# Constant fills off VectorE, query maxima split in PSUM, tails transposed by TensorE, and loads issued step by step in a fused attention and gated-MLP kernel

## The chip, the cores and the metric

One core of a Trainium2 chip. The metric is device time in microseconds (us) of one execution. A lower time is better. Executions of one kernel vary by a few per cent here, so each comparison below says how many runs stand behind it. A run is called slow when it is over 1.5% above the fastest run of its kernel; fast runs are compared with fast runs. Engines: PE is TensorE, PEld its weight loads, DVE VectorE, ACT ScalarE, POOL GpSimd, SP the sync engine, whose only work here is to issue DMA (a "q" behind a name is its queue of issues).

## The reference

Linear attention over 8 batches of 8 heads, 576 tokens of 64 elements, followed by a gated MLP whose gate mixes tokens.

```python
def phi(x):                                   # attention features
    proj = einsum('bhsd,df->bhsf', x, w_phi)  # 64 -> 128
    proj = proj - max(abs(proj), axis=-1)
    return concatenate([exp(proj), exp(-proj)], axis=-1)
q_p, k_p = phi(q), phi(k)
kv = einsum('bhsf,bhsd->bhfd', k_p, v);  z = sum(k_p, axis=2)
attn = (q_p @ kv) / (q_p @ z + 1e-6)
x = attn as (batch, token, head*64)           # 8 x 576 x 512
u, v = split(relu(x @ w_in));  v_n = layernorm(v)
v_s = einsum('ts,bsd->btd', w_spatial, v_n) + b_spatial
out = (u * v_s) @ w_out
```

## The kernel before

The 576 tokens of a head are 512 ("main") and 64 ("tail"). A **unit** is a pair of heads of one batch (main tokens), or the tails of two batches together (all eight heads). Unit 0 is the first pair of batch 0, unit 1 the first tail, units 2 to 4 the other pairs of batch 0. In step i the kernel works on several units at different stages and fills the gaps with MLP tasks from a queue, which is empty until batch 0 is through. Names of tiles below: k_tl, q_tl and v_tl are loaded tails, k_bf, q_bf and v_f loaded main tokens; kT and qT are their transposes (kT_t, qT_t for tails and kT_b, qT_b for a batch by DMA); mk and mq are the maxima, mhl a maximum in two bf16 parts and mT its transpose; kf and qf are the features (exponentials); em is exp of the key maxima, vs and vst are v and its tails scaled by em; vn and vnt are the normalized v of the MLP and of its tails (vnt has a row of ones, for the bias); xT is the transposed attention output; ob is an output buffer. In some views L61 stands for many places, since it is the line of the helper `pin`.

```python
def load_tail(g):                                  # both tails of a group
    ...
    for x, t in (("k", k), ("q", q)):
        for i in range(2):
            pin(nc.gpsimd.dma_start)(out=d[x][i*TL:(i+1)*TL], in_=tail_ap(t, 2*g + i))
        if 2*g >= XB:                              # all groups but the first
            d[x+"T"] = ld.tile([P, NP, P], BF16, tag=x+"T_t", ...)
            pin(nc.sync.dma_start_transpose)(out=d[x+"T"], in_=d[x]...)
    ...                                            # v by sync

def load(b):                                       # k and q by gpsimd, each with its DMA transpose
    alloc(b); load_heads(b, 0, H)
    load_v(b, nc.gpsimd if b < 2 else nc.sync)
...
for i in range(2):                                 # constants, before the loop
    t = cpool.tile([P, 2, 2, H, DA], BF16, name=f"vst{i}");  nc.vector.memset(t, 0.0)
    t = cpool.tile([P, 2, HALF], BF16, name=f"vnt{i}");      nc.any.memset(t, 0.0)
    ...
def a_queries(u):                                  # maxima of |q features| by VectorE, from PSUM
    u["mq"] = small.tile([P, H], FP32, tag="mq")
    for half in range(2):
        nc.vector.tensor_reduce(out=u["mq"][:, 4*half:4*half+4], in_=by_token(u["qT"], half), ...)
def a_split(u):                                    # fp32 maximum into two bf16 parts
    m = mhl[u["i"] % NM];  eng = nc.vector if u["i"] < EARLY else nc.gpsimd
    eng.tensor_copy(out=m[:, 0:H], in_=u["mq"])
    eng.tensor_tensor(out=m[:, H:2*H], in0=u["mq"], in1=m[:, 0:H], op=ALU.subtract)
...
ORDER = (("keys", 0.375), ("queries", 0), ("sums", 0), ("next", 0.125),
         ("attention", 0.5), ("features", 0), ("maxima", 0), ("out", 0))
RATE = 3.23;  CAP = 1.76                           # how much MLP work goes behind each stage
...
for i in range(NU + 4):
    u = unit(i);  step(i)
    if i == 0: load(1); load_weights()
    if u and u["pair"] and u["pj"] == NP-1 and u["b"]+2 < B: load(u["b"]+2)
    if u and u["pair"] and u["pj"] == TS and u["b"]%2 == TB and u["g"]+1 < G: load_tail(u["g"]+1)
```

Of the kernel before, what the change touches and what calls it, by code (L numbers as in the profile page):

```python
# [16 lines left out]
def kernel(  # L17
# [25 lines left out]
    NB = 4  # L43
# [16 lines left out]
    def pin(start):  # L60
        return lambda **kw: tc.keep_in_program_order(start(**kw))  # L61
# [12 lines left out]
    TS, TB = 1, 1  # L74
    XB = 2

    def load_tail(g):
        d = dict(
            q=ld.tile([P, H, D], BF16, tag="q_tl", name="q_tl", bufs=1),
            k=ld.tile([P, H, D], BF16, tag="k_tl", name="k_tl", bufs=1),  # L80
            v=ld.tile([P, H, D], FP32, tag="v_tl", name="v_tl", bufs=1),
        )
        gs[g] = d
        for x, t in (("k", k), ("q", q)):
            for i in range(2):
                pin(nc.gpsimd.dma_start)(out=d[x][i * TL:(i + 1) * TL], in_=tail_ap(t, 2 * g + i))
            if 2 * g >= XB:
                d[x + "T"] = ld.tile([P, NP, P], BF16, tag=x + "T_t", name=x + "T_t", bufs=1)
                pin(nc.sync.dma_start_transpose)(out=d[x + "T"], in_=d[x].rearrange("p h d -> p (h d)"))
        for i in range(2):  # L90
            pin(nc.sync.dma_start)(out=d["v"][i * TL:(i + 1) * TL], in_=tail_ap(v, 2 * g + i))

    def alloc(b):
        st[b] = dict(
            q=ld.tile([P, H, NB * D], BF16, tag="q_bf", name="q_bf", bufs=2),
            k=ld.tile([P, H, NB * D], BF16, tag="k_bf", name="k_bf", bufs=2),
            v=ld.tile([P, H * NB, D], FP32, tag="v_f", name="v_f"),
        )
        if b >= XB:
            for x in ("kT", "qT"):  # L100
                st[b][x] = ld.tile([P, 2 * H, P], BF16, tag=x + "_b", name=x + "_b", bufs=2)

    def load_heads(b, h0, n):
        d = st[b]
        for x, t in (("k", k), ("q", q)):
            src = d[x][:, h0:h0 + n]
            pin(nc.gpsimd.dma_start)(out=src, in_=main_ap(t, b, h0, n))
            if b >= XB:
                pin(nc.sync.dma_start_transpose)(out=d[x + "T"][:, 2 * h0:2 * (h0 + n), :],
                                            in_=src.rearrange("p h x -> p (h x)"))  # L110
# [4 lines left out]
    def load(b):  # L115
        alloc(b)
        load_heads(b, 0, H)
        load_v(b, nc.gpsimd if b < 2 else nc.sync)


    ident = cpool.tile([P, P], BF16)
    make_identity(nc, ident)
    alloc(0)
    for x, t in (("k", k), ("q", q)):
        first = s2.tile([P, 2, NB * D], FP32, tag="ob", name="first", bufs=4)
        nc.sync.dma_start(out=first, in_=main_ap(t, 0, 0, 2))
        nc.vector.tensor_copy(out=st[0][x][:, 0:2], in_=first)
    wphi2 = cpool.tile([P, 2 * F], BF16)
    nc.vector.memset(wphi2, 0.0)
    wphi_f = cpool.tile([P, F], FP32)  # L130
    for i in range(2):
        r = slice(i * D, (i + 1) * D)
        nc.sync.dma_start(out=wphi_f[r, :], in_=w_phi)
        nc.vector.tensor_copy(out=wphi2[r, i * F:(i + 1) * F], in_=wphi_f[r, :])
    load_tail(0)
    load_heads(0, 2, 2)
    load_v(0, nc.gpsimd)
    load_heads(0, 4, 4)
# [3 lines left out]
    w_spT = cpool.tile([P, NB + 2, S], BF16)  # L142
# [7 lines left out]
    def load_weights():  # L150
        pin(nc.gpsimd.dma_start)(out=w_in_bf, in_=moe_w_in.rearrange("(kc p) f -> p kc f", p=P))
        rows = moe_w_spatial[0:T0, :].rearrange("(p c) s -> p c s", c=NB)
        pin(nc.gpsimd.dma_start)(out=wsp, in_=rows[:, :, 0:T0])
        pin(nc.gpsimd.dma_start)(out=wspr, in_=rows[:, :, T0:S])
        pin(nc.gpsimd.dma_start)(out=wspt, in_=moe_w_spatial[T0:S, :])
        pin(nc.gpsimd.dma_start)(out=w_out_bf, in_=moe_w_out.rearrange("(kc p) f -> p kc f", p=P))


    sel1 = cpool.tile([P, H], BF16)
    sel = cpool.tile([P, H, F], BF16)  # L160
    nc.vector.tensor_tensor(out=sel1, in0=ident[:, 0:H], in1=ident[:, H:2 * H], op=ALU.add)
    nc.vector.tensor_scalar(out=sel, in0=sel1.unsqueeze(2).to_broadcast([P, H, F]), scalar1=-1.0,
                            scalar2=None, op0=ALU.mult)
    neghalf = cpool.tile([P, NB + 1], FP32)
    nc.vector.memset(neghalf, -0.5)


    NM = 3
    EARLY = 4
    XX = 9  # L170
    mhl, mT = [], []
    for i in range(NM):
        t = cpool.tile([P, P], BF16, name=f"mhl{i}")
        nc.vector.memset(t, 0.0)
        mhl.append(t)
        t = cpool.tile([P, P], BF16, name=f"mT{i}")
        nc.vector.memset(t, 0.0)
        mT.append(t)
    vst, vnt = [], []
    for i in range(2):  # L180
        t = cpool.tile([P, 2, 2, H, DA], BF16, name=f"vst{i}")
        nc.vector.memset(t, 0.0)
        vst.append(t)
        t = cpool.tile([P, 2, HALF], BF16, name=f"vnt{i}")
        nc.any.memset(t, 0.0)
        nc.any.memset(t[TL:TL + 1, 0, :], 1.0)
        nc.any.memset(t[0:1, 1, :], 1.0)
        vnt.append(t)
    nc.any.memset(w_spT[:, NB:NB + 2, :], 0.0)

    def transpose_spatial(i):
# [17 lines left out]
        for bl, row in ((0, TL), (1, 0)):  # L209
            for pos, c in enumerate(POS):  # L210
                nc.vector.tensor_copy(out=w_spT[row:row + 1, NB + bl, pos * P:(pos + 1) * P],
                                      in_=bsp_row[row:row + 1, bass.ds(c, P, step=NB)])
            nc.vector.tensor_copy(out=w_spT[row:row + 1, NB + bl, T0:S], in_=bsp_row[row:row + 1, T0:S])


    def a_transpose(u):
# [5 lines left out]
        for x, copy in (("k", nc.scalar.copy), ("q", nc.vector.tensor_copy)):  # L222
            pt = psum.tile([P, 4, P], BF16, tag="bank", name="pt")
            for j in range(4):
                if u["pair"]:
                    blk = src[x][:, 2 * u["pj"] + j // 2, (j % 2) * P:(j % 2 + 1) * P]
                else:
                    blk = src[x][:, 2 * j:2 * j + 2, :]
                nc.tensor.transpose(out=pt[:, j, :], in_=blk, identity=ident)
            u[x + "T"] = a1.tile([P, 4, P], BF16, tag=x + "T", name=x + "T", bufs=2 if x == "k" else 4)  # L230
            copy(out=u[x + "T"], in_=pt)
# [21 lines left out]
    def a_queries(u):  # L253
        u["mq"] = small.tile([P, H], FP32, tag="mq", name="mq")
        for half in range(2):
            pq = by_token(u["qT"], half)
            nc.vector.tensor_reduce(out=u["mq"][:, 4 * half:4 * half + 4], in_=pq, axis=AX.X, op=ALU.max,  # L257
                                    apply_absolute_value=True)

    def a_scale(u):  # L260
        em = small.tile([P, 2, H], FP32, tag="em", name="em")
# [10 lines left out]
        else:  # L272
            d = gs[u["g"]]
            vs = vst[u["g"] % 2]
            for bl in range(2):
                r = slice(bl * TL, (bl + 1) * TL)
                for s in range(2):
                    nc.gpsimd.tensor_tensor(out=vs[r, bl, s, :, 0:D], in0=d["v"][r],
                                            in1=em[r, s, :].unsqueeze(2).to_broadcast([TL, H, D]), op=ALU.mult)
                nc.gpsimd.tensor_copy(out=vs[r, bl, :, :, D:D + 1].rearrange("p i n o -> p i (n o)"), in_=em[r])  # L280
            d["vs"] = vs
            d["unit"] = u

    def a_split(u):
        m = mhl[u["i"] % NM]
        eng = nc.vector if u["i"] < EARLY else nc.gpsimd
        eng.tensor_copy(out=m[:, 0:H], in_=u["mq"])  # L287
        eng.tensor_tensor(out=m[:, H:2 * H], in0=u["mq"], in1=m[:, 0:H], op=ALU.subtract)
# [239 lines left out]
    def unit(i):  # L528
        return units[i] if 0 <= i < NU else None
# [3 lines left out]
    def b_tasks(b):  # L533
# [15 lines left out]
        if tail:  # L549
# [5 lines left out]
            for x in bls:  # L555
# [3 lines left out]
    ORDER = (("keys", 0.375), ("queries", 0), ("sums", 0), ("next", 0.125),  # L559
             ("attention", 0.5), ("features", 0), ("maxima", 0), ("out", 0))  # L560
    RATE = 3.23
    CAP = 1.76
# [10 lines left out]

    def lag(u, what):
        return (FIRST if u["pair"] and u["b"] == 0 or u["i"] == 1 else LAGS).get(what, 0)

    def step(i):
# [3 lines left out]
        for what, share in ORDER:  # L581
            for u in units[max(0, i - 5):i + 2]:
# [8 lines left out]
                elif what == "queries":  # L591
                    a_queries(u)
                    a_split(u)
# [23 lines left out]

    for i in range(NU + 4):
        u = unit(i)
        step(i)  # L620
        if i == 0:
            load(1)
            load_weights()
        if u and u["pair"] and u["pj"] == NP - 1 and u["b"] + 2 < B:
            load(u["b"] + 2)
        if u and u["pair"] and u["pj"] == TS and u["b"] % 2 == TB and u["g"] + 1 < G:
            load_tail(u["g"] + 1)
# [32 lines left out]
```

## Time and profile before

| | before |
|---|---|
| median of 3 runs | 302.22 us (300.67 to 305.91) |
| profiled span | 300.1 us |
| first product with w_in | 53.55 us |
| last group of tail products with w_out starts | 287.67 us |

The prediction below shows the busy times, the first windows and the main waits. Two more views will be compared. The timeline of VectorE, cut to the key maxima `mk` (start, length, engine, line, operation), is a clock of the start: one such group for each unit.

```profile
28.66 1.29 DVE L248 TENSOR_REDUCE mk<-ps 128x4 f32<-128x512 f32 x2
...
48.08 1.29 DVE L248 TENSOR_REDUCE mk<-ps 128x4 f32<-128x512 f32 x2
```

These are units 3 and 7. The view of DMA issues gives size and median time from issue to landing; the first piece of k behind the one that the sync queue loads (two heads, for unit 2) is this one:

```profile
k_bf<-in_k_dram POOLq DMA_DIRECT2D x1, 128.0 KB, 4.0
```

### The profile page before, as it was taken

How to read it: one execution, taken by the hardware profiler on the slowest of the kernel's cores; microseconds unless marked ns; L12 is line 12 of the kernel's file. 1: busy time of each engine (PE TensorE's matmuls, PEld its weight loads, DVE VectorE, ACT ScalarE, POOL GpSimd, SP SyncE). 2: the span in 40 equal slices, each digit the busy share in tenths (PEclk: the TensorE clock that was granted, in tenths of full speed). 3: DMA queues.
4: the chain of work that ended last, by engine and by line, in shares of the span. 5: the costliest groups of instructions: out<-in, count | busy, mean ns of one | idle time of the engine just before them, and what ended most of it. 6: DMA issues, size and time to landing. Idle time of an engine off the chain costs nothing.

```text
span 300.1 us, 7883 instructions
## 1 busy us (share of the span) xinstructions
PE 262.3 (87%) x3007; PEld 180.4 (60%) x3046; DVE 211.9 (71%) x512; ACT 224.1 (75%) x512; POOL 184.1 (61%) x324
## 2 busy tenths in 40 slices
PE   2356888999999999779999995979999999999983
PEld 1235777576766766556667673656767667545441
DVE  5999889797968877549697883656788864445610
ACT  4336899878699997769999675879999837566033
POOL 9398388589635998447879962814988430048300
PEclk9999999999999999999999997999999999999998
DMA  9999999909952899999612999999303202600026
GB/s 142 245 153 268 166 111 159 262 1 123 215 190 75 109 166 233 152 280 162 136 21 28 185 211 224 142 305 235 81 1 37 20 2 69 226 26 0 0 84 233
DMA packets 82906, 41.10 MB, mean 137 GB/s; under 512 B 53490, under 2 KB 77234, under 8 KB 82868
## 3 DMA queue, kind: packets, MB, share of 16 engines
q1 hardware_dynamic: 55524, 27.08, 41.9%
q0 software_dynamic: 27344, 13.51, 33.1%
q8 instruction: 24, 0.39, 0.6%
q14 instruction: 14, 0.11, 0.1%
HBM read 32.85 MB, written 9.44 MB: 141 GB/s over the span
## 4 chain that ended last, share of the span: by engine, by line
PE 56%; DVE 16%; ACT 14%; DMA 8%; issue 3%; SPq 1%; ACTq 0%; DVEq 0%
PE ps L476 9%; PE pv L402 7%; PE pu L455 6%; PE po L499 6%; PE ps L236 6%; DMA out_dram<-ob 5%; ACT kf L251 5%; PE pn L353 3%; DVE mk L248 3%; DVE mq L257 3%; PE pv L333 3%; ACT qf L320 3%; PE pq L303 3%; PE pq L307 3%; PE ps L477 2%
## 5 line engine op out<-in xcount | busy, mean ns | idle before, releaser
L251 ACT ACTIVATE kf<-ps 128x512 bf16<-128x512 f32 x144 | 76.8, 667 | 19.4 <-DVE mk L248 19.1
L320 ACT ACTIVATE qf<-pq 128x512 bf16<-128x512 f32 x128 | 68.0, 667 | 13.6 <-PE pq L307 13.6
L268 POOL TENSOR_TENSOR vs<-v_f,em 128x512 bf16<-128x512 f32 x64 | 65.6, 1047 | 15.7 <-ACT em L263 15.5
L248 DVE TENSOR_REDUCE mk<-ps 128x4 f32<-128x512 f32 x72 | 46.1, 678 | 9.5 <-PE ps L236 9.2
L257 DVE TENSOR_REDUCE mq<-ps 128x4 f32<-128x512 f32 x72 | 46.3, 679 | 3.1 <-PE ps L236 2.7
L501 ACT COPY ob<-po 128x512 f32<-128x512 f32 (+1 forms) x37 | 21.6, 597 | 25.7 <-PE po L499 17.2
L405 DVE BATCH_NORM_STATS2 stats<-vr 128x6 f32<-128x512 bf16 (+1 forms) x37 | 25.2, 685 | 17.6 <-ACT vr L404 17.5
L402 PE MATMUL pv<-w_in_bf,xT 128*128 128x512 bf16 x119 | 31.2, 379 | 2.2 <-DMA xT<-x 1.7
L476 PE MATMUL ps<-w_spT,vn 128*128 128x512 bf16 x117 | 32.3, 379 | 0.6
L455 PE MATMUL pu<-xT,w_in_bf 128*128 128x512 bf16 x120 | 30.8, 379 | 0.7 <-DVE mq L257 0.3
L307 PE MATMUL pq<-mT,sel 128*128 128x128 bf16 x256 | 30.7, 222 | 0.0
L499 PE MATMUL po<-w_out_bf,uT 128*128 128x512 bf16 x121 | 29.7, 379 | 0.4 <-issue 0.2
L479 DVE TENSOR_TENSOR uT<-ps,uT 128x512 bf16<-128x512 f32 x32 | 22.1, 691 | 11.0 <-PE ps L477 9.7
L307 PEld LDWEIGHTS <-sel 128*128 128x128 bf16 x256 | 25.4, 99 | 6.5 <-issue 2.2
L344 DVE TENSOR_TENSOR x<-pn,rc 128x256 bf16<-128x256 f32 x64 | 25.8, 419 | 1.0
L287 POOL CAST mhl<-mq 128x8 bf16<-128x8 f32 x32 | 6.2, 192 | 33.1 <-DVE mq L257 29.3
L404 ACT ACTIVATE vr<-pv 128x512 bf16<-128x512 f32 (+1 forms) x37 | 23.2, 680 | 4.2 <-PE pv L402 3.3
L333 PE MATMUL pv<-vs,kf 128*128 128x66 bf16 x512 | 25.0, 195 | 0.0
L419 POOL TENSOR_SCALAR vn<-vr,rs 128x512 bf16<-128x512 bf16 x32 | 24.3, 772 | 0.8
L333 PEld LDWEIGHTS <-kf 128*128 128x128 bf16 x512 | 23.9, 99 | 1.0
L353 PE MATMUL pn<-kv,qf 128*128 128x66 bf16 x512 | 22.2, 193 | 2.0 <-ACT kf L251 0.9
L353 PEld LDWEIGHTS <-qf 128*128 128x128 bf16 x512 | 19.4, 97 | 6.0 <-issue 2.5
(127 smaller groups left out, 547.5 us busy)
## 6 DMA issues: line engine op xcount, KB each, us to landing
out_dram<-ob SPq DMA_DIRECT2D x32, 256.0 KB, 2.7
v_f<-in_v_dram SPq DMA_DIRECT2D x6, 1024.0 KB, 6.8
k_bf<-in_k_dram POOLq DMA_DIRECT2D x7, 512.0 KB, 6.7
q_bf<-in_q_dram POOLq DMA_DIRECT2D x7, 512.0 KB, 8.3
v_f<-in_v_dram POOLq DMA_DIRECT2D x2, 1024.0 KB, 8.5
v_tl<-in_v_dram SPq DMA_DIRECT2D x8, 128.0 KB, 4.2
w_in_bf<-in_moe_w_in_dram POOLq DMA_DIRECT2D x1, 1024.0 KB, 12.5
out_dram<-ob SPq DMA_DIRECT2D x8, 128.0 KB, 2.9
```

The source lines that it names most:

```text
L248: nc.vector.tensor_reduce(out=u["mk"][:, hs], in_=pk, axis=AX.X, op=ALU.max, apply_absolute_value=True)
L251: nc.scalar.activation(out=u["kf"][:, s, hs, :], in_=pk, func=AF.Exp, bias=0.0, scale=sc)
L257: nc.vector.tensor_reduce(out=u["mq"][:, 4 * half:4 * half + 4], in_=pq, axis=AX.X, op=ALU.max, apply_absolute_value=True)
L268: nc.gpsimd.tensor_tensor(out=vs[:, s, :, 0:D], in0=st[u["b"]]["v"][:, pj * H:(pj + 1) * H, :], in1=em[:, s, :].unsqueeze(2).to_broadcast( ...
L307: nc.tensor.matmul(out=pq[:, 2 * par + x, :], lhsT=sel[:, j, :], rhs=m, start=False, stop=(x == 1))
L320: nc.scalar.activation(out=qf[:, s], in_=pq, func=AF.Exp, bias=0.0, scale=sc)
L333: nc.tensor.matmul(out=pv[:, hh, s, :], lhsT=u["kf"][:, s, 4 * hh + c, :], rhs=u["vs"][:, s, 4 * hh + c, :], start=(c == 0), stop=False)
L353: nc.tensor.matmul(out=pn[:, pos, :], lhsT=u["qf"][hh][:, s, pos, :], rhs=d["kv"][:, 2 * u["pj"] + hh, s, :], start=(s == 0), stop=(s == 1))
L402: nc.tensor.matmul(out=pv[r], lhsT=lhs(kc), rhs=w_in_bf[:, kc, HALF:DFF], start=(kc == 0), stop=(kc == KC - 1))
L455: nc.tensor.matmul(out=pu, lhsT=w_in_bf[:, kc, dc * P:(dc + 1) * P], rhs=d["xT"][:, kc, :], start=(kc == 0), stop=(kc == KC - 1))
L476: nc.tensor.matmul(out=ps, lhsT=d["vn"][:, sp, cs], rhs=w_spT[:, sp, 0:T0], start=(sp == 0), stop=False)
L499: nc.tensor.matmul(out=po[r], lhsT=lhs(dc), rhs=w_out_bf[:, dc, :], start=(dc == 0), stop=(dc == KC - 1))
```

## The change

The intent is to start earlier and to take waits off TensorE. The fills of vst and vnt and the bias rows go to ScalarE, while the first key evictions (units below 7) go to VectorE; the early query maxima are left in PSUM and split from there; tails are always transposed by TensorE; loads go out one or two a step, some steps ahead, and v of batches 0 and 1 comes by the sync queue; the filler's order and rates are new.

```diff
+    for x in ("k", "q"):                                  # casts of the first heads ahead of the fills
+        pin(nc.vector.tensor_copy)(out=st[0][x][:, 0:2], in_=first[x])
     for i in range(2):
         t = cpool.tile([P, 2, 2, H, DA], BF16, name=f"vst{i}")
-        nc.vector.memset(t, 0.0)
+        pin(nc.scalar.copy)(out=t..., in_=zero.to_broadcast([P, 4 * H * DA]))
         ...                                               # vnt and the bias rows likewise; wphi2 by ScalarE
+    load_v(0, nc.sync)
...
-        for x, copy in (("k", nc.scalar.copy), ("q", nc.vector.tensor_copy)):
+        for x, copy in (("k", nc.vector.tensor_copy if u["i"] < EK else nc.scalar.copy), ...):
...
     def a_queries(u):
+        m, early = mhl[u["i"] % NM], u["i"] < EARLY       # EARLY 4 -> 5
         for half in range(2):
             pq = by_token(u["qT"], half)
+            if early and half == 0:
+                mq = pq[:, 0, 0:H]                        # the maxima stay in PSUM
...
-            if 2 * g >= XB:
-                pin(nc.sync.dma_start_transpose)(out=d[x + "T"], in_=d[x]...)   # tails
...
-    ORDER = (("keys", 0.375), ("queries", 0), ("sums", 0), ("next", 0.125),
-             ("attention", 0.5), ("features", 0), ("maxima", 0), ("out", 0))
-    RATE = 3.23;  CAP = 1.76
+    ORDER = (("keys", 0.375), ("queries", 0.25), ("attention", 0), ("sums", 0.25),
+             ("next", 0.125), ("features", 0), ("out", 0), ("maxima", 0))
+    RATE = 3.12;  CAP = 2.11
...
+    at(1, load, "k", 1);  at(1, load, "q", 1);  at(1, load_v, 1, nc.sync)
+    at(2, load_weight, w_in_bf[:, :, HALF:DFF], ...);  at(3, ...);  at(4, ...)
+    for u in units:
+        if not u["pair"] and u["g"] > 0:                  # tails four and three steps ahead
+            at(u["i"] - AT, load_tail, "k", u["g"]); ...
+        if u["pair"] and u["pj"] == 0 and u["b"] > 1:     # k five, q and v four steps ahead
+            at(u["i"] - AB, load, "k", u["b"]); ...
+            at(u["i"] - XP, cross, u["b"])                # DMA transpose two steps ahead
```

## The prediction

> **What bounds the kernel now.** I read four views in this order: busy time per engine, the windows, the waits of TensorE, and the timeline of the first 30 us.
>
> The page's first part, and five stretches of the windows (columns: busy us with instruction counts, granted clock, DMA share, GB/s):
>
> ```profile
> PE 262.3 (87%) x3007; PEld 180.4 (60%) x3046; DVE 211.9 (71%) x512; ACT 224.1 (75%) x512; POOL 184.1 (61%) x324
> ```
>
> ```profile
> 0.00:10.00 10.00, 2.22 (x12) 1.19 (x12) 6.48 (x20) 3.07 (x4) 8.35 (x16) 1.00 1.05 161
> 10.00:20.00 10.00, 4.74 (x29) 3.41 (x29) 9.74 (x22) 4.92 (x14) 6.20 (x8) 1.00 1.13 193
> 20.00:30.00 10.00, 6.99 (x45) 5.32 (x46) 9.73 (x18) 5.38 (x14) 9.16 (x13) 1.00 1.17 252
> ...
> 120.00:130.00 10.00, 6.49 (x78) 4.47 (x77) 3.82 (x9) 5.76 (x14) 5.76 (x10) 1.00 1.45 167
> ...
> 180.00:190.00 10.00, 6.66 (x68) 4.54 (x71) 3.61 (x8) 5.73 (x14) 4.22 (x7) 0.83 1.35 212
> ```
>
> TensorE is the bound: adding the columns of all its matmuls at 2.4 per ns (a 512-column product starts every 0.216 us in dense stretches) gives about 240 us of work in a span of 300.1. The other 60 us are lost in four places. Up to 53.5 us, where the first product with w_in starts, TensorE does about 24 us of column work: 30 lost. The stretches 120 to 130 and 180 to 190 hold 5.8 and 5.4 us of work: about 9 lost. The last 10 us are mostly the final copies and stores: about 10 lost. Some 10 more are spread out. In the first 30 us VectorE, not TensorE, is full: 6.48 + 9.74 + 9.73 us busy.
>
> The waits of TensorE (waiter, line, what it waited for: us in total, times, longest):
>
> ```profile
> PE ps L236 <- ACT kT L231: 7.1, 4, 3.6
> PE ps L236 <- DMA kT_t<-k_tl: 5.1, 2, 3.4
> ...
> PE ps L236 <- DVE qT L231: 3.4, 1, 3.4
> ...
> PE pv L402 <- DMA xT<-x: 1.7, 1, 1.7
> ```
>
> The kT_t lines are the DMA-transposed tails; they explain both dips. The first and third are the start. The timeline of the start shows why VectorE is full (start, length, engine):
>
> ```profile
> 6.17 0.94 DVE L182 MEMSET vst<- 128x1056 uint32 x1 [0.28 <-issue]
> ...
> 14.12 0.27 DVE L211 CAST w_spT<-bsp_row 1x128 bf16<-1x128 f32 x1
> ...
> 14.99 2.06 POOL L268 TENSOR_TENSOR vs<-v_f,em 128x512 bf16<-128x512 f32 x2
> 15.06 1.03 DVE L213 CAST w_spT<-bsp_row 1x64 bf16<-1x64 f32 x1
> ...
> 19.83 1.27 DVE L287 CAST mhl<-mq 128x8 bf16<-128x8 f32 x1
> ```
>
> Constants and bias rows stand ahead of, or between, the maxima that release ScalarE and TensorE. A cast of half the size took 1.03 instead of 0.27 us beside a GpSimd product, and an 8-column cast took 1.27 instead of the 0.17 of its first use.
>
> **What the Trainium skill says.** "SBUF — State Buffer", section "Who interferes with whom": copies and casts in SBUF may take a port pair shared with GpSimd as an exclusive lock, and a VectorE operation with two SBUF inputs contends with GpSimd's reads. The 0.27 to 1.03 above agrees. At 19.83 GpSimd was issuing loads rather than multiplying, which the same page's section "SBUF: two separate sides" describes as needing that pair too; this fits, though the trace alone does not prove it. "TensorE: Matmul & The Clock Gate", Part 1: the array runs at half rate until a window of about 3.4 us has been busy and falls back after an idle one. The trace agrees: up to 32 us one 256-column product with its two 128-column ones repeats every 0.42 us, from 36 us every 0.22; after the 3.4 us wait at 180 the four 512-column products are 0.43 us apart and the window's clock is 0.83. "DMA: Bandwidth & Descriptors", section "Issuing engines are not separate DMA queues": moving v to the sync queue buys no bandwidth, only issue time. Here a v issue costs GpSimd 0.91 to 0.95 us twice, and the DMA share is at its top in the first 60 us anyway.
>
> **The change part by part.**
>
> *Start.* Taken from VectorE ahead of the maxima of unit 3 (28.66 us): two vst fills 1.88, four vnt fills 1.92, bias rows 5.7 (four at 0.27, and 1.03, 1.05, 1.55, 1.03), and about 2.9 of contention on the two splits and the mT copy behind them, because the split now reads PSUM. That is 12.4. Added: four kT copies of 0.42 = 1.7, and one fill of w_spT, 0.55. Net 10 us less on VectorE. Not all of it is gained, since other engines take over. ScalarE issues two loads (0.6 each), loads its table (1.28), fills vst (2112 columns, estimate 1.95 from 0.67 for 576), and only then writes wphi2: first products near 5.8 us against 5.95. It then fills vnt, vst, vnt (4.4 us), so the first kf starts at about 10.2 instead of 11.37. From there a step costs ScalarE 2.07 + 0.33, plus 2.07 for qf once that begins. Key products wait for banks freed by kf. The first sums need the tail's vst, which GpSimd finishes near 17.4 (vs from 12.6, 2.1 + 0.3, then 2.1 + 0.3). With half-clock products (about 4 us of transposes, features and products behind these sums) the maxima of unit 3 come at about 22 us, 6.5 earlier.
>
> From there VectorE's sum per step sets the pace. The same sum (1.28 + 1.28 + copies + rc and x 1.0 + xT 0.43 + mT 0.2) reproduces the kernel before within 0.5 us: unit 3 at 28.66, then 34.2, 38.2, 43.6 computed against 34.64, 38.63, 43.50. In the changed order steps 3 to 6 come to 5.5, 4.4, 5.5, 5.1 (kT copies and VectorE splits added): unit 7 at 42.5 against 48.08. **Gain 5.6.**
>
> *Tails by TensorE.* The two waits for kT_t, 5.1 us, go, and with them the slow clock behind them, about 10 us x (1 - 0.83) = 1.7. **Gain 6.8.** Cost: 24 transposes of 128 columns, 1.3 us of TensorE on the bound; three copies of 0.6 on ScalarE and three of 0.42 on VectorE lie beside it. **Loss 1.3.**
>
> *Loads by step.* Before, the sync queue waits 75.8 us for k loads, so outputs and xT transposes queue behind these: ScalarE waits 6.9 us for output buffers, TensorE 1.7 for xT. Now loads are issued four to five steps ahead and transposed two steps ahead, so the head of that queue is seldom blocked. Only TensorE's 1.7 is on the bound. Against it, kT_b and qT_b take 7.1 and 6.5 us to land one after the other, about two steps of 6.4 us: little slack. I count **gain 1.5, loss 0.6**.
>
> *Order, RATE, CAP.* Work is moved, not removed. The lower RATE leaves more for the dense end. I count zero.
>
> Sum: 302.2 - 5.6 - 6.8 + 1.3 - 1.5 + 0.6 = **290.2 us**, 4% faster.
>
> **The rivals.** *A: ScalarE becomes the bound.* For: it is 10.00 of 10 busy in several later windows, and takes some 5 us of fills at the start and three tail copies, while its kT copies fall from nine to five. Against: TensorE is at 9.9 there too, and in the first 20 us ScalarE is busy only 8 of 20. If true, the start gains only 2 to 3 us and the middle loses 2: about 295. *B: late loads take the place of the waits removed.* For: k and q of batch 1 stand behind products on GpSimd (issue near 17.3 instead of 13.95), v of batch 1 now competes earlier, and kT_b has two steps. Against: they are needed only near 28, and 6.7 to 8.3 us to land gives about 26. If true, waits of 1 to 3 us in several batches: 295 to 299. *C: the clock makes it larger.* A denser start warms the array several us earlier, and the spread losses of 10 us shrink with fills after queries and sums: 281 to 285. *D: the start is hidden later*, because TensorE has a queue of work. Against: the queue is empty until batch 0 is done at 53 us, so earlier is earlier for everything; I give it little.
>
> **Range and chances.** A or B put it at 295 to 299, C at 281 to 285; the main line is 290. The range 281 to 298 holds eight in ten. Two per cent faster means under 296.2, which needs half of the sum: I give 0.86. Within 2%: 0.12. Slower: 0.02, for B in every batch.
>
> **What would show it.** Right: unit 3's maxima near 22 us and the first w_in product near 48 instead of 53.5; mhl casts of VectorE all near 0.2 us; no kT_t line among TensorE's waits; clock near 1.00 in every window; TensorE's busy time little changed with 24 more matmuls; the end unchanged. Wrong: a kf start later than 11.4 us or ScalarE full from 10 to 50 us (A); TensorE waiting for kT_b, qT_b or k_bf by several us (B). If the first w_in product is not earlier, the main step has failed, whatever the total.

## The result, and the profile after

| | before | after |
|---|---|---|
| median | 301.84 us (4 runs, 300.67 to 305.91) | 291.18 us (4 runs, 288.2 to 293.32) |
| profiled span | 300.1 us | 286.4 us |
| first product with w_in | 53.55 us | 47.06 us |
| last group of tail products with w_out starts | 287.67 us | 274.09 us |

The ratio of the fast runs is 0.9587, 95% interval 0.9501 to 0.9672: faster. A ratio here is the mean time of one kernel's fast runs over that of the other's in the same rounds, so it is not quite the ratio of the medians. Two of the four runs after were slow in state (292.59 and 293.32), and the mean of the fast two is 288.99.

The page's first part, and the granted clock in 40 slices:

```profile
PE 261.6 (91%) x3070; PEld 178.6 (62%) x3070; DVE 201.8 (70%) x509; ACT 229.3 (80%) x517; POOL 182.2 (64%) x320
...
PEclk9999999999999999999999999999999999999999
```

TensorE is as busy as before with some more matmuls, in a span 13.7 us shorter. The same stretches of the windows as in the prediction:

```profile
0.00:10.00 10.00, 3.08 (x16) 1.81 (x16) 5.26 (x19) 6.08 (x7) 6.74 (x14) 1.00 0.88 189
10.00:20.00 10.00, 5.03 (x31) 3.52 (x32) 5.28 (x16) 6.07 (x15) 2.88 (x4) 1.00 1.24 209
20.00:30.00 10.00, 8.36 (x130) 6.97 (x128) 9.16 (x26) 8.59 (x21) 9.85 (x14) 1.00 0.91 116
120.00:130.00 10.00, 10.00 (x104) 6.89 (x103) 8.05 (x21) 9.90 (x24) 8.36 (x13) 1.00 1.06 229
180.00:190.00 10.00, 9.11 (x129) 6.27 (x128) 6.89 (x19) 8.34 (x22) 5.39 (x11) 1.00 1.16 307
```

The two dips of the middle are gone. The clock column is no witness for the start: it reads 1.00 there, yet four 256-column products take some 1.06 us up to 19.64 us and 0.60 from 23.73 on (TensorE's timeline); before, it was 1.06 up to 28.77 and 0.60 from 34.09. From 10 to 20 us, though, no engine is full: VectorE has 5.28 us of work, ScalarE 6.07, GpSimd 2.88. Something else holds the start. The waits of TensorE name it:

```profile
PE pt L225 <- DVE k_bf L61: 4.3, 1, 4.3
PE pt L225 <- DMA k_tl<-in_k_dram: 3.4, 1, 3.4
PE ps L232 <- ACT wphi L61: 1.8, 1, 1.8
PE pt L225 <- DMA q_tl<-in_q_dram: 1.8, 1, 1.8
PE ps L232 <- DMA qT_b<-q_bf: 1.4, 1, 1.4
```

No kT_t line is left. New are waits for k_tl, q_tl and, through `wphi`, for the load of w_phi: all early loads. In the view of DMA issues the same first piece of k now stands so, and the v loads so:

```profile
k_bf<-in_k_dram POOLq DMA_DIRECT2D x1, 128.0 KB, 12.2
...
v_f<-in_v_dram SPq DMA_DIRECT2D x8, 1024.0 KB, 10.7
```

The piece takes 12.2 us to land, where it took 4.0. Two loads of v, 1 MB each, are issued by the sync queue at 1.74 and 5.04 us, the first of them before GpSimd has issued k_bf at 4.50. So it looks as if part of the expected gain at the start was spent on late loads (x_v01 below tests it), and yet the first product with w_in is 6.5 us earlier. Units 3 and 7 in VectorE's timeline:

```profile
24.23 1.29 DVE L244 TENSOR_REDUCE mk<-ps 128x4 f32<-128x512 f32 x2
...
41.94 1.27 DVE L244 TENSOR_REDUCE mk<-ps 128x4 f32<-128x512 f32 x2
```

Of the 13.6 us by which the last stage starts earlier, 6.5 are there at the first product with w_in and 7.1 come between it and the last stage.

### The profile page after: what moved, and what is told of

Same layout as the page of the kernel before. It is cut to its first block, busy times and chain, and to the rows that moved or that the text cites. A ratio compares the mean times of both kernels' runs of the same rounds, so it can differ in the third digit from the quotient of the medians.

```text
span 286.4 us, 7965 instructions
## 1 busy us (share of the span) xinstructions
PE 261.6 (91%) x3070; PEld 178.6 (62%) x3070; DVE 201.8 (70%) x509; ACT 229.3 (80%) x517; POOL 182.2 (64%) x320
## 4 chain that ended last, share of the span: by engine, by line
PE 61%; ACT 14%; DVE 11%; DMA 9%; POOL 2%; issue 2%; ACTq 0%; SPq 0%; POOLq 0%; DVEq 0%
PE pv L403 10%; PE ps L477 8%; PE po L500 7%; PE pu L456 7%; PE ps L232 5%; ACT qf L321 5%; ACT kf L247 5%; PE pv L334 4%; DMA q_tl<-in_q_dram 4%; PE pn L354 4%; DMA out_dram<-ob 3%; PE pq L308 3%; PE pq L304 3%; DVE mk L244 3%; PE ps L478 2%; DVE mq L258 2%
## 5 line engine op out<-in xcount | busy, mean ns | idle before, releaser
L247 ACT ACTIVATE kf<-ps 128x512 bf16<-128x512 f32 x144 | 77.7, 692 | 5.6 <-DVE mk L244 5.4
L258 DVE TENSOR_REDUCE mq<-ps 128x4 f32<-128x512 f32 x62 | 39.9, 681 | 4.2 <-PE ps L232 3.4
L456 PE MATMUL pu<-xT,w_in_bf 128*128 128x512 bf16 x128 | 31.6, 379 | 0.0
L500 PE MATMUL po<-w_out_bf,uT 128*128 128x512 bf16 x128 | 30.4, 379 | 0.0
L308 PE MATMUL pq<-mT,sel 128*128 128x128 bf16 x256 | 30.0, 219 | 0.0
L354 PEld LDWEIGHTS <-qf 128*128 128x128 bf16 x512 | 20.4, 97 | 8.2 <-issue 1.7
L345 DVE TENSOR_TENSOR x<-pn,rc 128x256 bf16<-128x256 f32 x64 | 25.0, 418 | 0.5
L334 PEld LDWEIGHTS <-kf 128*128 128x128 bf16 x512 | 21.7, 97 | 1.8 <-issue 0.9
L304 PE MATMUL pq<-qT_b,wphi 128*128 128x256 bf16 x96 | 22.4, 273 | 0.0
```

Source lines behind the costliest of these rows:

```text
L247: nc.scalar.activation(out=u["kf"][:, s, hs, :], in_=pk, func=AF.Exp, bias=0.0, scale=sc)
L258: nc.vector.tensor_reduce(out=mq[:, 4 * half:4 * half + 4], in_=pq, axis=AX.X, op=ALU.max, apply_absolute_value=True)
L308: nc.tensor.matmul(out=pq[:, 2 * par + x, :], lhsT=sel[:, j, :], rhs=m, start=False, stop=(x == 1))
L334: nc.tensor.matmul(out=pv[:, hh, s, :], lhsT=u["kf"][:, s, 4 * hh + c, :], rhs=u["vs"][:, s, 4 * hh + c, :], start=(c == 0), stop=False)
L354: nc.tensor.matmul(out=pn[:, pos, :], lhsT=u["qf"][hh][:, s, pos, :], rhs=d["kv"][:, 2 * u["pj"] + hh, s, :], start=(s == 0), stop=(s == 1))
L456: nc.tensor.matmul(out=pu, lhsT=w_in_bf[:, kc, dc * P:(dc + 1) * P], rhs=d["xT"][:, kc, :], start=(kc == 0), stop=(kc == KC - 1))
```

## The experiments

Three calls of four kernels, each with 5 rounds, and each call on another chip; the medians of the kernel before, 301.76, 301.83 and 301.51, say that the chips agree. The changed kernel itself ran again in the first call only. Each kernel's profile is one of its runs. "Mean" is the mean of its fast runs, "median" that of all six (eleven for the kernel before). Line numbers shift by a few between kernels.

| kernel | mean, us (fast runs) | median, us | ratio to before | first w_in product, us |
|---|---|---|---|---|
| before, first call | 299.43 (3 of 11) | 301.76 | | 53.55 |
| a_control: the changed kernel again | 290.52 (3) | 293.63 | 0.973 (0.956 to 0.990) | 47.9 |
| x_tails: tails by DMA | 295.36 (5) | 296.18 | 0.986 (0.974 to 0.999) | 48.8 |
| x_v01: v(0), v(1) by GpSimd | 287.48 (6) | 287.48 | 0.960 (0.952 to 0.968) | 43.5 |
| b_tails: before, tails by TensorE | 299.82 (6) | 299.86 | 1.001 (0.994 to 1.009) | 53.2 |
| before, second call | 301.35 (10 of 11) | 301.83 | | |
| x_consts: fills on VectorE | 289.27 (5) | 289.74 | 0.960 (0.954 to 0.965) | 45.7 |
| x_split: maxima through SBUF | 292.64 (4) | 293.46 | 0.971 (0.965 to 0.977) | 49.1 (slow run) |
| x_order: old order and rates | 296.10 (6) | 295.80 | 0.982 (0.978 to 0.987) | 49.0 |
| x_sched: old load issue | 291.00 (5) | 291.42 | 0.966 (0.961 to 0.972) | 46.0 |
| before, third call | 301.01 (8 of 11) | 301.51 | | |
| b_order: before, new order | 303.83 (6) | 303.85 | 1.010 (1.005 to 1.016) | 53.4 |
| b_tails_order: both | 295.95 (3) | 298.19 | 0.980 (0.973 to 0.988) | 50.5 |
| b_start: before, new start | 297.52 (5) | 297.72 | 0.989 (0.984 to 0.994) | 47.9 |
| x_best: x_v01, further changed | 285.94 (4) | 286.41 | 0.951 (0.946 to 0.955) | 43.3 |

In the first call one run of before at 297.03 made all but two others count as slow, so the ratios of that call are to an unusually low mean; there I also compare medians. The changed kernel itself scatters most: 288.71 to 297.28 in six runs.

### a_control: the anchor

No edit.

> The changed kernel again, as the reference point on this chip. 0.955 to 0.965 of the kernel before (288 to 292 us); the first product with w_in near 47 us.

It came at 290.52 in the fast runs, with the k_tl wait at 5.8 in its profile. The differences "undone" below are to this 290.52; since x_consts, x_split, x_order and x_sched ran in the next call, about 1.5 us of them could be noise (the fast runs of the result had 288.99).

### x_v01: are the late loads caused by v on the sync queue?

```diff
-    load_v(0, nc.sync)
     for x in ("k", "q", "v"):
         load_tail(x, 0)
     load("k", 0, 2, 2)
     load("q", 0, 2, 2)
+    load_v(0, nc.gpsimd)
...
-    at(1, load_v, 1, nc.sync)
+    at(1, load_v, 1, nc.gpsimd)
```

> The changed kernel with v of batches 0 and 1 issued by GpSimd again, behind the small k and q loads (v of batch 0) and behind k and q of batch 1. If v, issued first on the sync queue, delayed the tails and w_phi in the changed kernel (k_tl landed at 12.8, TensorE waited 3.4 + 1.8 for tails and 1.8 for wphi): tails land near 8 us, those waits shrink by 4 to 6 us, the first w_in product comes 3 to 5 us earlier, total 3 to 5 us less. If the loads are simply limited by the sum of bytes, or ScalarE's fills set the pace (kf from 11.6): under 1.5 us less.

All six runs were fast and within 285.85 to 288.95: 3.0 us less than the control's fast runs in the same call, and 1.5 less than the 288.99. The first piece of k, the key maxima of unit 3, and the largest new wait of TensorE (views of DMA issues, VectorE's timeline, waits):

```profile
k_bf<-in_k_dram POOLq DMA_DIRECT2D x1, 128.0 KB, 5.1
```

```profile
20.64 1.29 DVE L244 TENSOR_REDUCE mk<-ps 128x4 f32<-128x512 f32 x2 [0.28 <-PE ps L232]
```

```profile
PE pv L336 <- POOL vst L289: 2.7, 1, 2.7
```

The piece lands after 5.1 us instead of 12.2, unit 3 starts 3.6 us earlier than in the profile after, and the first product with w_in comes at 43.5. So it is shown that the early v by the sync queue delayed the small loads beside it, and that this cost 1.5 to 3 us of time. The edit also puts v behind the first small loads; whether the queue or the order of issue does it was not tested apart. The scatter is not explained by it: x_order keeps v on the sync queue and has six fast runs within 1.6 us, and x_best has v on GpSimd and two slow runs. A wait for the scaled tail of v (vst) takes up a part of what was freed, and more goes later: from the first product with w_in to the last group of tail products with w_out, x_v01's profile has 229.6 us and the control's 226.7, with one stretch at a lower clock (windows of x_v01):

```profile
190.00:195.00 5.00, 5.00 (x37) 2.51 (x36) 3.45 (x8) 5.00 (x14) 1.29 (x2) 0.72 1.17 217
```

### x_tails and b_tails: what are the tails worth?

Undone in the changed kernel (x_tails), and done alone in the kernel before (b_tails):

```diff
+            at(u["i"] - XP, cross_tail, u["g"])   # x_tails: DMA transposes two steps ahead
...
-            if 2 * g >= XB:                       # b_tails
+            if False:
```

> The changed kernel, but the tails of batches 2 to 7 are transposed by DMA again, issued two steps ahead of use. If the transfer itself is what TensorE waited for (the prediction's step): the two kT_t waits of 5.1 us and 1.7 us of slow clock come back, 1.3 us of transposes go: 5.5 us slower than the changed kernel. If the waits came from late tail loads and a blocked sync queue, which the new load schedule cures anyway: no kT_t wait over 0.5 us, and the time equal to the changed kernel or 1 us below it.

> The kernel before with one thing changed: tails of batches 2 to 7 transposed by TensorE. If TensorE's waits for kT_t were on the path: 5.1 + 1.7 - 1.3 = 5.5 us less than before, ratio 0.982. If another wait (output buffers, xT, k loads in the sync queue) takes their place: under 2 us less.

Undone, it costs 4.8 us in the same call, close to the prediction's net 5.5. But the wait for kT_t did not come back. Waits of TensorE and of ScalarE from 60 to 285 us (the profiled run, 297.61, is the second longest of the five fast ones, which go from 293.35 to 297.63, so its waits may be larger than most):

```profile
PE ps L238 <- ACT ob L508: 2.6, 2, 2.3
PE pt L299 <- ACT ob L508: 2.0, 1, 2.0
...
PE ps L238 <- DMA qT_t<-q_tl: 0.8, 1, 0.8
```

```profile
ACT ob L508 <- DMA out_dram<-ob: 9.5, 4, 4.6
```

TensorE waits for banks that ScalarE should empty, ScalarE waits 9.5 us for output buffers (3.2 in the kernel after), and these are free only once their stores have gone out of the sync queue, in which the tail transposes now stand waiting for k_tl and q_tl (17.5 and 12.0 us of that queue's waits). By this trace the cost is the queue, not the transposed data; a run with the tail transposes on another queue was not made.

Alone (b_tails) the tails bring little: 1.9 us by the medians, nothing by the ratio. The kT_t waits are gone, and this takes their place:

```profile
PE pt L229 <- DMA q_tl<-in_q_dram: 2.2, 1, 2.2
PE ps L236 <- ACT ob L501: 1.4, 2, 1.1
PE pt L229 <- ACT em L263: 1.0, 1, 1.0
```

GpSimd issues k_tl and q_tl only at 111.9 and 112.6 us there, and they are needed near 117 to 119. From 120 to 125 us the clock is then 0.74: an estimate of 1.3 us (5 us x 0.26) is lost to it on top of the waits, so that much of what kT_t had cost is paid again.

### x_consts and x_split: what made the start earlier?

```diff
-        pin(nc.scalar.copy)(out=t.rearrange(...), in_=zero.to_broadcast(...))   # x_consts: vst and vnt
+        pin(nc.vector.memset)(t, 0.0)
...
-            if early and half == 0:                                             # x_split
+            if False:                             # mq is an SBUF tile; VectorE still splits it
```

> The changed kernel with the large constant fills (vst, vnt) back on VectorE, the first of them before the casts of the first heads, the rest after; everything else as changed. T1 (the prediction's sum for the start): VectorE has about 5.7 us more to do in the first 16 us, and the early units start later, first w_in product 2 to 4 us later than in the control (47 to 48), time 2 to 4 us longer than the control's fast runs (290.5). T2 (what the trace after showed: units 1 and 2 wait for the late k_tl and 2-head loads anyhow, mk starts 8.3, 16.4, 19.8): the fills lie beside that wait and ScalarE is freed for the first exponentials, so the first w_in product stays within 1 us of 47.5 and the time within 1.5 us of the control.

> The changed kernel with the early query maxima reduced into SBUF as before and split from there by VectorE; one part undone. T1 (prediction: the splits cost 1.27 us each on VectorE only while GpSimd writes SBUF): the casts to mhl are again near 1 us while GpSimd scales, the first w_in product 1 to 3 us later, time plus 1 to 3 us. T2 (the late loads set the pace of the first units; the splits are not on that path): casts slower but first w_in product and time within 1 us of the control.

Putting the fills back on VectorE, which also takes them off ScalarE, costs nothing measurable (289.27, against 290.52 and 288.99). Unit 0's maxima come 1.9 us later than in the profile after, at 10.21, and then unit 1 waits for its data all the same (`PE pt L226 <- DMA q_tl<-in_q_dram: 3.2, 1, 3.2`). The first product with w_in is at 45.7. With early loads of x_v01's kind the fills might matter; that was not run.

Splitting from SBUF costs 2.1 to 3.7 us (292.64 against 290.52 and 288.99). The profile of x_split fell into a slow run, so of it I use only the durations. VectorE's two operations on mhl (operation, count, min/median/max ns):

```profile
L261 DVE CAST mhl<-mq x5: 148/161/1016, 13.8 to 33.3; 128x8 bf16<-128x8 f32 x5
L262 DVE TENSOR_TENSOR mhl<-mq,mhl x5: 157/868/915, 16.6 to 33.7; 128x8 bf16<-128x8 f32 x5
```

After the change all ten of these took 153 to 167 ns; the subtraction:

```profile
L262 DVE TENSOR_TENSOR mhl<-ps,mhl x5: 153/156/167, 17.0 to 32.6; 128x8 bf16<-128x8 f32 x5
```

With both inputs in SBUF four of the five subtractions took 0.87 to 0.92 us. Three of these ran beside a product on GpSimd and one, at 33.66, beside its load issues; the fifth, at 16.65 with GpSimd idle, took 0.16. That fits what the Trainium skill says in "SBUF — State Buffer", section "Who interferes with whom", of a VectorE instruction with two SBUF inputs beside a GpSimd instruction that reads SBUF (the one beside load issues is not covered by that sentence); the subtraction after the change has one of them in PSUM.

### x_order and b_order: does the filler's order count?

```diff
-    ORDER = (("keys", 0.375), ("queries", 0.25), ("attention", 0), ("sums", 0.25), ...   # x_order
-    RATE = 3.12;  CAP = 2.11
+    ORDER = (("keys", 0.375), ("queries", 0), ("sums", 0), ("next", 0.125), ("attention", 0.5), ...
+    RATE = 3.23;  CAP = 1.76
```

b_order is the reverse edit in the kernel before.

> The changed kernel with the filler order and rates of before (ORDER, RATE 3.23, CAP 1.76). T1 (prediction: these count for zero): time within 1.5 us of the control, first w_in product within 1.5 us of 47.5, no new wait above 2 us on TensorE. T2 (the new order is part of the gain, tuned to the new start): 2 to 5 us longer, with the steps of the first nine units longer by 0.3 us or more, or new TensorE waits in the middle.

> The kernel before with only the filler order and rates of the changed kernel (ORDER, RATE 3.12, CAP 2.11). Undone in the changed kernel, the order cost about 5 us (295.8 beside 290 to 291), where the prediction gave it zero. T1 (the order is a gain by itself: fewer places in a step where TensorE waits for an eviction): 3 to 6 us faster than before (296 to 299), the kT_t waits unchanged at 4 to 5. T2 (the order only pays together with the other parts, since it fits their start and loads): within 2 us of before (300 to 304).

Undone, the order costs 5.6 us, as much as the tails. No single wait explains it. The stage from the first product with w_in to the last group of tail products with w_out, of a_control and then of x_order (windows, columns as in the prediction: busy times, clock, DMA share, GB/s):

```profile
47.90:274.62 226.72, 222.94 (x2616) 150.49 (x2616) 165.10 (x402) 186.25 (x426) 145.92 (x262) 1.00 0.73 128
```

```profile
49.00:281.46 232.46, 225.31 (x2615) 150.90 (x2616) 165.99 (x401) 186.35 (x425) 143.29 (x260) 0.99 0.74 123
```

Of the 5.7 us more, TensorE is idle for 3.4 (7.15 against 3.78) and busy for 2.4. The largest part in one place is this dip; the windows' line for 140 to 145 us, of a_control and then of x_order:

```profile
140.00:145.00 5.00, 5.00 (x59) 3.17 (x58) 4.45 (x11) 5.00 (x13) 2.72 (x7) 1.00 0.72 72
```

```profile
140.00:145.00 5.00, 3.68 (x14) 1.47 (x15) 0.64 (x2) 3.32 (x9) 3.15 (x9) 0.66 1.10 180
```

In x_order a wait of 1.9 us for a copy by ScalarE ends at 140.8, and one of 0.5 us at 141.8. The clock of this stretch is 0.66: four 512-column products take 1.89 us to run instead of 1.04, and an estimate of 1.7 us (5 us x 0.34) is lost to the clock. That is not what makes the kernel slow as a whole: the other five runs of x_order had mean clocks of 0.991 to 0.994 instead of 0.985 and still took 295.47 to 297.08, and x_v01 has such a stretch too and is 8.6 us faster. So what is shown is that the old order costs 5.6 us and that TensorE is idle more under it; which of ORDER, RATE and CAP does it, and by which way, stays open.

Alone in the kernel before, the same order does harm: 2.3 us by the medians. Its tails' wait has grown from 5.1 to 7.0 us:

```profile
PE ps L236 <- DMA kT_t<-k_tl: 7.0, 2, 4.1
```

So the order is no gain by itself. That it pays where the tails are no longer waited for is a guess from this line, which the next runs support only weakly.

### b_tails_order and b_start: parts added up

b_tails_order has the edits of b_tails and b_order together. b_start has the whole start (fills, splits, early key evictions, first loads) with the old order, the old load issue and the tails by DMA; v of batches 0 and 1 stays on GpSimd.

> The kernel before with the tails by TensorE and the new filler order, start and load issue as before. T1 (parts add: tails alone about 2, order about 5): 294 to 296, no kT_t wait, q_tl wait of about 2 near 118 left. T2 (the order makes the tails' gain of 5.5 real, because the old order let TensorE run dry after the late q_tl): 290 to 293. T3 (no addition): 298 to 301.

> The kernel before with only the start of the changed one (fills off VectorE, maxima split in PSUM, early key evictions by VectorE, first loads reordered), with the old order, old load issue and DMA-transposed tails. Prediction's step: first w_in product at about 48 instead of 53.5, time 5.6 us less (296). Rival from the last runs (x_sched, with v off the sync queue, had its first w_in product at 46, the fills themselves cost nothing): first w_in product at 46 to 47, but of the 6 to 7 us saved there 2 or more are lost again at the unchanged kT_t waits, which come at a fixed distance after the loads: 297 to 299.

Tails and order together: 295.95 against 301.01 in the fast runs, 5.1 us less, though three of six runs were slow and the medians differ by only 3.3. Their separate effects, 1.9 less and 2.3 more, would give nothing. Among what is left are waits for the sync queue: the line below is one wait of 4.1 us, in the window of 140 to 160 us where TensorE falls to 15.70 of 20.

```profile
PE pv L402 <- DMA xT<-x: 4.1, 1, 4.1
```

The start alone: 3.5 us less, with the first product with w_in at 47.9 and a profiled span 4.9 shorter. So a start that is 5.6 us earlier reaches the end for the most part. kT_t costs 3.8 us and xT 3.1 there, together as much as the 5.1 and 1.7 before.

### x_sched: what is the issue by steps worth?

```diff
-    at(1, load, "k", 1);  at(1, load, "q", 1);  at(1, load_v, 1, nc.sync)
-    at(2, load_weight, ...);  at(3, ...);  at(4, ...)
+    at(0, load, "k", 1);  at(0, load, "q", 1);  at(0, load_v, 1, nc.gpsimd)
+    at(0, load_weight, ...)                       # all weights
...                                                # k, q, transposes, v of b+2 at the end of batch b; tails at pair 1
```

> The changed kernel with the load issue of before: k, q and v of the next batch together at the end of a batch, all weights together after step 0 on GpSimd, v of batches 0 and 1 on GpSimd, tails at pair 1 of odd batches; tails still transposed by TensorE. T1 (prediction: the issue by steps is worth a net 0.9): within 2 us of the control. T2 (tails by TensorE alone gained nothing, because k_tl and q_tl were issued too late for it; the early issue is what pays in the middle): 4 to 7 us longer than the control, with PE waits for q_tl or k_tl of 2 us or more near 118 and 190 as in the kernel before with the tails alone, although the start gains from v being off the sync queue (first w_in product 44 to 47).

It lies 0.5 us above the control's 290.52 and 2.0 above the 288.99: the prediction's net 0.9 holds, and my newer theory, which expected 4 to 7, fell. But the net hides two larger terms. x_sched has v on GpSimd, as x_v01 has, and the two differ by 3.5 us (291.00 against 287.48, from different calls). So the issue by steps gains some 3.5 us and v on the sync queue gives most of it back (1.5 to 3.0). One of the things gained shows as TensorE's largest wait in x_sched, where eight load issues stand in front of the scaling on GpSimd:

```profile
PE pv L336 <- POOL vst L289: 4.7, 1, 4.7
```

### x_best: a further step

```diff
-    load_v(0, nc.gpsimd)                           # x_v01
+    load_v(0, nc.gpsimd, 0, 2)                     # ahead of the k and q pieces; the other six heads behind
...
-            pin(nc.scalar.copy)(out=t[:, bl, :], in_=ident[:, row:row + 1].to_broadcast([P, HALF]))
+        pin(nc.gpsimd.memset)(t, 0.0)              # vnt, and its row of ones, by GpSimd; vst1 at step 8
```

> x_v01 (287.5) with the second vst fill moved to GpSimd at step 8, vnt filled by GpSimd in its idle time near 9 us, and v of batch 0 loaded in two pieces, the first two heads ahead of the k and q pieces. If the first exponentials are held by ScalarE's fills and vst by the late v_f (13.3 us): kf starts at about 7 instead of 9.7, the 2.7 us vst wait shrinks below 1, first w_in product 41 to 42.5 instead of 43.5, time 285.5 to 286.5. If the pace of units 1 to 6 is set by ScalarE and VectorE anyway (both near 10.00 from 30 on), within 0.7 us of x_v01.

ScalarE's first exponentials did start at 7.11 instead of 9.66, but vst was ready at 17.7 (17.6 in x_v01), and the first product with w_in came at 43.3. GpSimd's timeline shows what ate the gain:

```profile
11.25 1.98 POOL L61 MEMSET vnt<- 1x512 bf16 x3
13.20 1.03 POOL L275 TENSOR_TENSOR vs<-v_f,em 128x512 bf16<-128x512 f32 x1
14.29 1.08 POOL L61 MEMSET vnt<- 1x512 bf16 x2
```

A row of ones on a single partition still costs GpSimd 0.51 to 0.52 us, and 3.1 us of fills (the two groups above: four rows and one whole tile) stand among the scalings. That is my own mistake in this edit, and it can be mended. The fast runs are 1.5 us below those of x_v01 and the medians 1.1, but from different calls, with two slow runs of six: whether x_best beats x_v01 is not settled. Both beat the kernel before and the changed kernel.

## Why the prediction was right or wrong

The time was right: 290.2 predicted, 291.18 measured as the median and 288.99 as the mean of the fast runs, within the range. The steps did not all hold.

**Start (5.6 us).** Right in size: the first product with w_in came at 47.06 where "near 48" was predicted, and b_start passes 3.5 to 4.9 us of it to the end. The way there was not as worked out. Unit 3 started at 24.23, not near 22, because rival B, which I looked for at batch 1 and later, happened in the first 15 us: v on the sync queue made the k and q pieces and the tails late. In exchange steps 3 to 6 took 4.9, 3.7, 4.7 and 4.4 us, 2.8 less in sum than worked out. The two errors nearly cancel, which is luck. The sum of 12.4 us was itself too high: the first vst fill, at 1.61 us, ended ahead of an idle time of 1.13 us in which VectorE waited for the first load, and of the contention the cast of 1.27 us at 19.83 and the mT copy of 1.21 us at 19.90 overlap and were counted twice. Of the 12.4 us taken from VectorE, the fills (3.8) were worth nothing in x_consts; the split in PSUM was worth 2.1 to 3.7 us in x_split, more than any other part tested at the start. The bias rows and the key evictions were not tested apart. (The 1.95 us for a vst fill, as measured, does not follow from the 0.67 for 576 columns that the prediction names.)

**Tails by TensorE (5.5 net).** Right as a part of the whole (4.8 undone). All marks came as said: no kT_t line, clock near full. The reading behind it was half right: kT_t does not "explain both dips", since in the one of 120 to 130 us a wait of 1.71 us for kT_t is joined by one of 1.75 for xT. As a part by itself the gain was wrong: alone it gave 1.9 at most, since q_tl is then waited for. And undone it costs by another way, the blocked sync queue.

**Loads by step (0.9 net).** Right in sum, but as a balance of a gain of about 3.5 us, taken for 1.5, and a loss of 1.5 to 3.0, taken for 0.6: luck in part.

**Order, RATE, CAP (zero).** This is the step that failed. "Work is moved, not removed" is true, yet undone it costs 5.6 us: in the profiles TensorE is idle 3.4 us longer in the stage with the MLP, and some 1.7 us go to a lower clock behind one of the waits. Why the old order leaves it idle is open.

**Rivals.** A did not happen: ScalarE had 6.07 us of work from 10 to 20 us. The kf start was at 11.58 instead of 10.2, which was A's mark, but not from ScalarE being full: a 1.94 us wait for the load of w_phi stands ahead of it. C's clock was as full as it said, and its earlier warm array came too (full rate by 23.73 instead of 34.09 us); the total brought no more than the sum, but the short steps 3 to 6 may be C's. That was not tested. D fell with b_start.

**Why the sum still fits.** Undone one by one, fills, split, order, load issue and tails cost -1.3, 2.1, 5.6, 0.5 and 4.8 us against the control: 11.7 in sum, near the whole. Done one by one in the kernel before, start, tails and order give 3.5, 1.9 and -2.3: 3.1 in sum, and the issue by steps was not done alone. The parts seem to remove waits that stand in for one another, as q_tl stands in for kT_t in b_tails; that this holds for the whole is argued and not shown. I had no number for that, so the sum was partly luck.

## What to carry to other kernels

Test a bundle both ways, each part done alone and each undone: here three of its four parts alone gave 3 us in sum, and the whole 11. When large loads are moved to another queue, look at what becomes of the small ones that the first units need, and let the small ones be issued first. A change in the order of work that removes none can still count: look at how long the matmul engine is idle in the stage (here 7.2 against 3.8 us), and at the clock behind the waits. And before a lower clock is called the cause, compare it with the clocks and times of the other runs.

## What the Trainium skill lacked or had wrong

- "DMA: Bandwidth & Descriptors", section "Anatomy of one DMA — SWDGE (gpsimd) path", gives about 2.0 us plus the bytes at 436 GB/s for one DMA: for 128 KB that is an estimate of 2.3 us. Here such a load took 4.0 us in the kernel before, 5.1 in x_v01 and 12.2 after the change, with two 1 MB loads of the sync queue issued about it. I found no figure there for a small load beside large ones.
- The same page, section "Issuing engines are not separate DMA queues", says that issuing on several engines only saves issue time. It does not say that moving large loads ahead of small ones in this way can cost: 1.5 to 3.0 us between the changed kernel and x_v01.
- No page that I used puts a number on what a DMA transpose that waits for its source costs the stores behind it on the same issuing engine: from 60 to 285 us ScalarE waits 9.5 us for output buffers in x_tails, 3.2 in the kernel after.
- "TensorE: Matmul & The Clock Gate", Part 1, states a fall to half rate after an idle window of about 3.4 us, which agrees with a clock of 0.83 after a 3.4 us wait in the kernel before. It gives no figure for a window that is idle in part: in x_order waits of only 1.9 and 0.5 us close together came with a stretch at 0.66, while waits of 1.71 and 1.75 us between 120 and 130 us in the kernel before left the clock at 1.00.
- None of the pages that I used warns of fills on one partition: in x_best 512 elements on one partition took GpSimd 0.51 to 0.52 us, half of what 1024 elements on each of 128 partitions took (1.0 us): half the elements of a partition took half the time, whatever the number of partitions.
